# Forty-six chunks of 502 or 504 columns in place of fifty of 470 or 423 in a spectral layer and network on one Trainium2 core

## The chip, the cores and the metric

The kernel runs on one core of a Trainium2 chip. The metric is device time in microseconds (us), the median of several executions. The engines are TensorE (PE, its weight loads apart as PEld), VectorE (DVE), ScalarE (ACT), GpSimd (POOL) and the queue of SyncE (SP), which issues most DMAs.

## What is computed

For eight batches of 3008 rows by 256, a real Fourier transform along the rows, a complex linear map with a soft threshold, the transform back, and then a network on each of the 24064 rows:

```python
    X = np.fft.rfft(x, axis=1)
    Yr = Xr @ w_r - Xi @ w_i + b_r
    Yi = Xr @ w_i + Xi @ w_r + b_i
    Yr = np.sign(Yr) * np.maximum(np.abs(Yr) - lam, 0.0)
    Yi = np.sign(Yi) * np.maximum(np.abs(Yi) - lam, 0.0)
    y = np.fft.irfft(Y, n=x.shape[1], axis=1)
    ...
    h = x @ w_in                 # (24064, 256) @ (256, 2048)
    g = h - np.tanh(h)
    return g @ w_out             # (24064, 2048) @ (2048, 256)
```

## The kernel before

The transform of 3008 = 64 x 47 is done by matmuls in stages. Per batch: forward DFT blocks over 47 (`Stacked`: a load `xt`, the split `xs`, matmul L301 into `ps_f`, a copy `st`, a store `a`), then twelve units of the spectrum (`Spectrum`: a load `at`, the DFT over 64 at L360, the linear map at L380, the threshold on DVE, the inverse DFT over 64 at L426 to L428, a store `z`). The last inverse DFT, over 47, belongs to the network's input. Its work comes in groups of five columns of 24 frequencies (`groups`; each batch has 25 such groups and one of three, 208 in all), and a group turns into 5 x 23.5 columns of the network.

Network rows lie along the columns. A `Chunk` c has four consecutive groups, whichever batch they are of: 470 columns, or 423 (padded to 424) where the short group is among them; 52 chunks. For a chunk, `load` brings `zin`, `wave` does the last DFT (L579, into `ps_i`), `fold` makes `yt` from sums and differences (ACT `odd`, two DVE instructions), and `halves` splits `yt` into a rounded part `yh` (ACT, L599) and its rest `yl` (DVE, L600), for each of the two halves t of the 256 features.

The network is 16 steps f per chunk. A step has `up` (L608: six matmuls of 128x128 weights into a bank `h`: low weights by yh, high weights by yh and by yl, for t of 0 and 1), then ACT `th` = tanh(h), DVE `g` = h - th, ACT `gh`, DVE `gl`, and `down` (L639: six matmuls, accumulated over the 16 steps into two banks `o`). `up` runs two steps ahead of `down` (`AHEAD`), and PE's other work goes between. After the last step `store` copies `o` to `ot` and out.

The order: the first batch and 23 network steps of chunks 0 and 1, which alternate, are written out by hand, from `keep_warm` at the start (matmuls that keep PE busy) on. Everything after that is a plan in slots, one per network step: `plan_stacked` and `plan_spectrum` put each batch's stages at slots counted back from the step at which its first chunk is due, and a chunk's `load`, `time` (wave and fold) and `halves` get slots 2, 8 to 12 and one later. Within this part the framework may still move an instruction ahead on its engine where its inputs and buffers allow. The four banks of `ps_f` are shared by DFT work, and while chunk 1 runs, its two `o` are among them. `zin` has two buffers, as have `xt`, `yh` and `yl`.

Of the kernel before, what the change touches and what calls it, by code (L numbers as in the profile page):

```python
# [10 lines left out]
F32 = mybir.dt.float32  # L11
# [67 lines left out]
def spectral_ffn(ctx, tc, x, w_r, w_i, b_r, b_i, w_in, w_out, x_twice, f1, f1s, f2, i1, i2, out):  # L79
    nc = tc.nc  # L80
# [4 lines left out]
    CT = 470  # L85
# [448 lines left out]
    pieces = [(b, g) for b in range(B) for g in range(NG)]  # L534
# [5 lines left out]
    class Chunk:  # L540
        def __init__(self, c):
            self.c, self.out = c, sizes[c] * 47
            self.n = self.out + self.out % 2
            self.groups = members[c]
# [4 lines left out]
        def load(self):  # L549
            self.tile()  # L550
            k = 0
            while k < len(self.groups):
                b, g = self.groups[k]
                n = sum(q[0] == b and groups[q[1]] == groups[g] for q in self.groups[k:])
# [10 lines left out]
        def time(self, t):  # L565
            self.wave(t)
            self.fold(t)

        def wave(self, t):
            if t == 0:  # L570
                self.yh = work.tile([P, 2, PITCH], F32R, name="yh", tag="yh")
                self.yl = work.tile([P, 2, PITCH], F32R, name="yl", tag="yl")
                self.ps, self.y = {}, {}
            ps = self.ps[t] = ps_f.tile([P, 512], F32, name="ps_i2", tag="f")
            at = 0
            for k, (_, g) in enumerate(self.groups):
                m = groups[g] * NJ
                turn = (g % 2 if m == GR else 2) * GR
                nc.tensor.matmul(  # L579
                    ps[:, at:at + m], self.zt[:m, k, t * P:(t + 1) * P], i2t[:m, turn:turn + m], start=True, stop=True,  # L580
                )
                at += m

        def fold(self, t):
            n = self.n
            v = self.ps[t][:, :sizes[self.c] * 2 * NJ].rearrange("p (n r c) -> p n r c", r=2, c=NJ)
            odd = work.tile([P, D], F32, name="odd", tag="odd")
            ov = odd[:, :sizes[self.c] * NJ].rearrange("p (n c) -> p n c", c=NJ)
# [4 lines left out]
            yv = y[:, :self.out].rearrange("p (n c) -> p n c", c=47)  # L593
            nc.vector.tensor_tensor(out=yv[:, :, :NJ], in0=v[:, :, 0], in1=ov, op=ALU.add)
            nc.vector.tensor_tensor(out=yv[:, :, NJ:], in0=v[:, :, 0, 1:], in1=ov[:, :, 1:], op=ALU.subtract)

        def halves(self, t):
            n, y = self.n, self.y[t]
            nc.scalar.copy(out=self.yh[:, t, :n], in_=y[:, :n])  # L599
            nc.vector.tensor_tensor(out=self.yl[:, t, :n], in0=y[:, :n], in1=self.yh[:, t, :n].bitcast(F32), op=ALU.subtract)  # L600

        def up(self, f, between=()):
# [41 lines left out]
        def store(self):  # L644
            n = self.n
            ot = work.tile([P, 2, 512], F32, name="ot", tag="ot", bufs=1)
            if self.c == NCH - 1:
                lo, n, half = begin[self.c] * 47, self.out, self.n // 2
# [8 lines left out]
            lo, n = begin[self.c] * 47, self.out  # L657
# [5 lines left out]
    with tc.manual_schedule(engines={E.PE, E.Activation, E.DVE, E.Pool, E.SP}):  # L663
# [5 lines left out]
        def keep_warm(n):  # L669
            idle = ps_h.tile([P, 512], F32, name="idle", tag="h")  # L670
            for _ in range(n):
                nc.tensor.matmul(idle, warm[:, :P], warm, start=True, stop=True)

        keep_warm(8)
# [23 lines left out]
        keep_warm(25)  # L698
# [94 lines left out]
        for c in range(2):  # L793
            chunks[c].load_part(LATE, GR)
# [32 lines left out]
        for c in range(2):  # L827
            for t in range(2):
                chunks[c].time(t)
# [61 lines left out]
    def plan_spectrum(units, start, each, ahead, lag, rest):  # L891
        for jp, s in enumerate(units):
            at = start + int(jp * each)
            early = at - jp % 2 * each if units is not second else at
# [12 lines left out]
    whole = set()  # L907
    plan_stacked(1, 25, 1.75, 3, 2 * LOOK)
    plan_spectrum(second, 46, 2.95, 5, 2, 0)
    for b in range(2, B):  # L910
        end = NF * (next(c for c in range(NCH) if begin[c] + sizes[c] > b * 2 * NP) - 1)
        plan_stacked(b, end - 103, 1.75, 3)
        plan_spectrum([Spectrum(b, jp) for jp in range(NJ // 2)], end - 66, 5, 5, 2, 2)
    for c in range(2, NCH):
        at = NF * (c - 1)
        put(at + {2: 9, 6: 6}.get(c, 2), chunks[c].load)
# [50 lines left out]
```

## Time and profile before

| | us |
|---|---|
| median of 3 runs | 2639.81 |
| lowest, highest | 2638.63, 2640.34 |
| span of the profiled execution | 2637.2 |
| PE busy | 2629.1 |
| PEld busy | 2382.4 |
| DVE busy | 1872.5 |
| ACT busy | 1511.3 |
| POOL busy | 115.5 |

The span goes from the first to the last instruction of the profiled execution; the runs' times contain a little more around it. Busy time is a union of instruction times. Since matmuls are pipelined, the duration of one (370 ns for 470 columns) is more than its share of PE's time, which is the distance from its start to the next start.

### The profile page before, as it was taken

The page shows a single profiled execution, that of the slowest core. Times are in us where ns is not written, and L with a number is a line of the kernel's source. Part 1 is how long each engine was busy: PE and PEld are TensorE (multiplying, and loading weights), DVE is VectorE, ACT ScalarE, POOL GpSimd, SP SyncE. Part 2 cuts the span into 40 slices and gives each one's busy share as a digit, 9 for nine tenths or more (in the row PEclk, how much of TensorE's full clock was granted, in tenths as well). Part 3 has the DMA queues.
Part 4 walks back from the last instruction along what each step waited for, and adds up shares of the span by engine and source line. Part 5 has one row for each costly group of instructions (what it writes and reads, how often), then busy time and mean ns, then how long its engine had stood idle before and what let it go on. Part 6 is the DMA issues. An engine that isn't in the chain of part 4 may idle for free.

```text
span 2637.2 us, 38594 instructions
## 1 busy us (share of the span) xinstructions
PE 2629.1 (100%) x14098; PEld 2382.4 (90%) x14098; DVE 1872.5 (71%) x3431; ACT 1511.3 (57%) x2958; POOL 115.5 (4%) x131
## 2 busy tenths in 40 slices
PE   9999999999999999999999999999999999999999
PEld 7789999999999998999999999999999899999888
DVE  5896887677767776767776777667777677755555
ACT  4675558555665556755576555675558555545444
POOL 2110000000000000010000000000000000000000
PEclk9999999999999999999999999999999999999999
DMA  7543326322462213632155221462316422111000
GB/s 240 171 141 92 79 69 193 77 65 62 123 163 69 69 43 80 180 80 67 47 153 138 72 64 38 117 160 59 78 40 180 103 71 63 32 28 29 22 15 15
DMA packets 157543, 236.70 MB, mean 90 GB/s; under 512 B 12561, under 2 KB 108585, under 8 KB 157353
## 3 DMA queue, kind: packets, MB, share of 16 engines
q1 hardware_dynamic: 146025, 213.79, 28.2%
q0 software_dynamic: 11328, 20.45, 5.2%
q8 instruction: 111, 1.82, 0.3%
q14 instruction: 79, 0.65, 0.1%
HBM read 138.77 MB, written 95.42 MB: 89 GB/s over the span
## 4 chain that ended last, share of the span: by engine, by line
PE 96%; DVE 2%; DMA 1%; ACT 1%; issue 0%; SPq 0%; DVEq 0%; ACTq 0%
PE o L639 38%; PE h L608 38%; PE ps_v L380 5%; PE ps_i L579 3%; PE ps_f L360 3%; PE ps_t L380 2%; PE ps_f L301 2%; PE ps_i L428 1%; PE ps_i L427 1%; PE ps_i L426 1%; PE ps_v L482 1%; DMA xt<-in_x 1%; DVE gl L626 0%; PE ps_i L530 0%; ACT gh L623 0%
## 5 line engine op out<-in xcount | busy, mean ns | idle before, releaser
L620 DVE TENSOR_TENSOR g<-h,th 128x470 f32<-128x470 f32 (+1 forms) x832 | 530.8, 638 | 389.0 <-ACT th L617 381.8
L617 ACT ACTIVATE th<-h 128x470 f32<-128x470 f32 (+1 forms) x832 | 462.7, 556 | 588.0 <-PE h L608 584.6
L626 DVE TENSOR_TENSOR gl<-g,gh 128x470 fp32r<-128x470 f32 (+1 forms) x832 | 534.2, 642 | 260.5 <-ACT gh L623 250.2
L623 ACT CAST gh<-g 128x470 fp32r<-128x470 f32 (+1 forms) x832 | 483.7, 581 | 365.7 <-DVE g L620 362.1
L639 PE MATMUL o<-gh,wout_l 128*128 128x470 f32 (+1 forms) x1664 | 624.7, 375 | 0.0
L639 PE MATMUL o<-gl,wout_h 128*128 128x470 f32 (+1 forms) x1664 | 616.8, 371 | 0.0
L639 PE MATMUL o<-gh,wout_h 128*128 128x470 f32 (+1 forms) x1664 | 616.0, 370 | 0.0
L608 PE MATMUL h<-yh,win_l 128*128 128x470 f32 (+1 forms) x1664 | 483.4, 371 | 0.8 <-DVE g L620 0.6
L608 PE MATMUL h<-yl,win_h 128*128 128x470 f32 (+1 forms) x1664 | 482.1, 370 | 0.0
L608 PE MATMUL h<-yh,win_h 128*128 128x470 f32 (+1 forms) x1664 | 480.2, 370 | 0.0
L608 PEld LDWEIGHTS h<-yh,win_l 128*128 128x128 f32 x1664 | 311.7, 188 | 37.7 <-DVE g L620 3.0
L639 PEld LDWEIGHTS o<-gl,wout_h 128*128 128x128 f32 x1664 | 312.7, 188 | 36.3 <-DVE gl L626 1.8
L608 PEld LDWEIGHTS h<-yl,win_h 128*128 128x128 f32 x1664 | 312.6, 188 | 32.6 <-DVE yl L600 0.3
L639 PEld LDWEIGHTS o<-gh,wout_h 128*128 128x128 f32 x1664 | 313.2, 188 | 31.8
L608 PEld LDWEIGHTS h<-yh,win_h 128*128 128x128 f32 x1664 | 312.6, 188 | 32.4
L639 PEld LDWEIGHTS o<-gh,wout_l 128*128 128x128 f32 x1664 | 313.5, 188 | 31.3 <-DVE ot L656 0.2
L296 DVE TENSOR_TENSOR xs<-xt,xs 47x512 fp32r<-47x512 f32 x208 | 139.8, 681 | 41.2 <-ACT xs L295 38.6
L411 DVE TENSOR_TENSOR y<-tb,ps_v 64x256 f32<-64x256 f32 x384 | 160.2, 417 | 7.1 <-ACT tb L498 3.1
L347 POOL DMA_DIRECT2D at<-a x84 | 79.8, 991 | 1780.6 <-DMA at<-a 879.6
L295 ACT CAST xs<-xt 94x512 fp32r<-94x512 f32 x208 | 127.9, 626 | 9.6 <-DMA xt<-in_x_twice 9.3
L304 ACT COPY st<-ps_f 96x512 f32<-96x512 f32 x208 | 117.7, 578 | 1.1 <-PE ps_f L301 1.0
L579 PEld LDWEIGHTS ps_i<-i,zin 120*128 120x128 f32 (+1 forms) x832 | 99.4, 192 | 3.3 <-ACT st L304 0.9
(114 smaller groups left out, 2440.3 us busy)
## 6 DMA issues: line engine op xcount, KB each, us to landing
xt<-in_x_twice SPq DMA_DIRECT2D x104, 384.0 KB
a<-st SPq DMA_DIRECT2D x104, 384.0 KB
at<-a SPq DMA_DIRECT2D x96, 256.0 KB
z<-zo SPq DMA_DIRECT2D x93, 240.0 KB
out<-ot SPq DMA_DIRECT2D x44, 470.0 KB
zin<-z SPq DMA_DIRECT2D x42, 480.0 KB
at<-a POOLq DMA_DIRECT2D x72, 256.0 KB, 5.1
turn<-in_i SPq DMA_DIRECT2D x96, 128.0 KB
```

The source lines that it names most:

```text
L295: nc.scalar.copy(out=xs, in_=src)
L296: nc.vector.tensor_tensor(out=xs[:47], in0=src[:47], in1=xs[:47].bitcast(F32), op=ALU.subtract)
L304: nc.scalar.copy(out=self.st[:, 2 * q:2 * q + 2, :], in_=pv)
L380: nc.tensor.matmul(dst, lhs[:, t], rhs[:, t, :], start=n == 0, stop=n == 5)
L411: nc.vector.tensor_tensor(out=y[ri * 64:(ri + 1) * 64, jj, :], in0=common(jj, ri), in1=self.side(ri)[jj * 64:(jj + 1) * 64], op=ALU.add,)
L579: nc.tensor.matmul(ps[:, at:at + m], self.zt[:m, k, t * P:(t + 1) * P], i2t[:m, turn:turn + m], start=True, stop=True,)
L608: nc.tensor.matmul(h[:, :n], lhs[:, t, f * P:(f + 1) * P], rhs[:, t, :n], start=k == 0, stop=k == 5)
L617: nc.scalar.activation(out=th[:, :n], in_=h[:, :n], func=AF.Tanh)
L620: nc.vector.tensor_tensor(out=g[:, :n], in0=h[:, :n], in1=th[:, :n], op=ALU.subtract)
L623: nc.scalar.copy(out=gh[:, :n], in_=g[:, :n])
L626: nc.vector.tensor_tensor(out=gl[:, :n], in0=g[:, :n], in1=gh[:, :n].bitcast(F32), op=ALU.subtract)
L639: nc.tensor.matmul(self.o[t][:, :n], lhs[:, f, t * P:(t + 1) * P], rhs[:, :n], start=f == 0 and k == 0, stop=f == NF - 1 and k == 2,)
```

## The change

From chunk 2 on, chunks are no longer made of whole groups. The last DFT's work is now a class of its own, `Wave`: up to four groups of one batch, seven waves per batch, 56 in all (the seventh has two groups, 188 columns). The 23124 columns after the first two chunks are divided evenly by `edge` into 46 chunks of 502 or 504. A chunk takes its columns from the two or three waves that it overlaps (`parts`), and `halves` makes `yh` and `yl` piece by piece. A wave's `yt` lives until the next chunk has taken the rest of it, so waves take turns over four homes, three of them buffers of the weight preparation. A wave is loaded at slot 2 of the chunk that first needs it, or four slots earlier if another follows for the same chunk. The batches' stages are planned against the load of the batch's first wave, with forward blocks every 1.6 slots for 1.75 and units every 4.6 for 5. The warm-up of 25 matmuls of 512 columns becomes 40 of mixed shapes with as many columns in all. `th` and `g` get 512 columns of room.

```diff
-    members = [pieces[k:k + 4] for k in range(0, len(pieces), 4)]
+    members = [[(b, g) for g in range(k, min(k + 4, NG))] for b in range(B) for k in range(0, NG, 4)]
     sizes = [sum(groups[g] for _, g in m) // 2 for m in members]
-    begin = [sum(sizes[:c]) for c in range(len(sizes))]
-    NCH = len(sizes)
+    begin = [47 * sum(sizes[:w]) for w in range(len(sizes) + 1)]
+    NCH = 48
+    rest = begin[-1] - begin[2]
+    edge = begin[:2] + [begin[2] + 2 * round(rest * c / (2 * (NCH - 2))) for c in range(NCH - 1)]
...
+    class Wave:
+        def __init__(self, w):
+            self.w, self.groups = w, members[w]
+            self.home = ((work, "yt"), (cvt, "w_f"), (cvt, "w_s"), (cvt, "w_m"))[w % 4 if w > 1 else 0]
...
-            y = self.y[t] = work.tile([P, PITCH], F32, name="yt", tag="yt")
-            if n > self.out:
-                nc.gpsimd.memset(y[:, self.out:n], 0.0)
+            pool, tag = self.home
+            y = self.y[t] = pool.tile([P, PITCH], F32, name="yt", tag=tag)
...
+    class Chunk:
+        def __init__(self, c):
+            self.c, self.lo, self.hi = c, edge[c], edge[c + 1]
+            self.n = self.hi - self.lo
+            self.parts = [w for w in waves if begin[w.w] < self.hi and begin[w.w + 1] > self.lo]
...
         def halves(self, t):
-            n, y = self.n, self.y[t]
-            nc.scalar.copy(out=self.yh[:, t, :n], in_=y[:, :n])
-            nc.vector.tensor_tensor(out=self.yl[:, t, :n], in0=y[:, :n], in1=self.yh[:, t, :n].bitcast(F32), op=ALU.subtract)
+            for w in self.parts:
+                lo, hi = max(self.lo, begin[w.w]), min(self.hi, begin[w.w + 1])
+                y = w.y[t][:, lo - begin[w.w]:hi - begin[w.w]]
+                yh, yl = (v[:, t, lo - self.lo:hi - self.lo] for v in (self.yh, self.yl))
+                nc.scalar.copy(out=yh, in_=y)
+                nc.vector.tensor_tensor(out=yl, in0=y, in1=yh.bitcast(F32), op=ALU.subtract)
...
-        keep_warm(25)
+        keep_warm((8, P, P, 512), (16, P, P, P), (5, 94, 96, 512), (5, 94, P, 512), (6, P, P, D))
...
+    whole, asked, new = set(), {}, {}
+    for c in range(2, NCH):
+        new[c] = [w for w in chunks[c].parts if w.w > 1 and w not in asked]
+        last, apart = (9, 1) if c == 2 else (2, 4)
+        for k, w in enumerate(reversed(new[c])):
+            asked[w] = NF * (c - 1) + last - apart * k
...
-        plan_stacked(b, end - 103, 1.75, 3)
-        plan_spectrum([Spectrum(b, jp) for jp in range(NJ // 2)], end - 66, 5, 5, 2, 2)
+        end = asked[waves[b * len(waves) // B]] - 2
+        plan_stacked(b, end - 95, 1.6, 3)
+        plan_spectrum([Spectrum(b, jp) for jp in range(NJ // 2)], end - 61, 4.6, 5, 2, 2)
...
-        slot = at + (12 if c == 2 else next((k for k in range(8, 13) if at + k in whole), 10))
+        last = NF * (c - 1) + 12
+        for w in new[c]:
+            put(asked[w], w.load)
+            near = range(asked[w] + 6, min(asked[w] + 11, last + 1))
+            slot = asked[w] + 3 if c == 2 else next((k for k in near if k in whole), near[len(near) // 2])
+            for t in range(2):
+                put(slot, w.time, t)
         for t in range(2):
-            put(slot, chunks[c].time, t)
             put(slot + 1, chunks[c].halves, t)
```

Three places in the order of instructions. The first is on PE, in the last steps of chunks 0 and 1, where the last DFT for chunk 2 is done. Names: `h` and `o` are the network's banks, `ps_f` a forward block, `ps_i` the last DFT. Before:

```order
L608 MATMUL h<-yl,win_h 128x470 x2
L301 MATMUL ps_f_1808<-xs,f_stack 96x512
L579 MATMUL ps_i_1817<-i_261,zin 128x120 x4
L639 MATMUL o_1045<-gh,wout_l 128x470
L579 MATMUL ps_i_1827<-i_261,zin 128x120 x4
L639 MATMUL o_1045<-gh,wout_h 128x470
```

And now:

```order
L300 MATMUL ps_f_1795<-xs,f_stack 96x512
L571 MATMUL ps_i_1804<-i_276,zin 128x120 x4
L645 MATMUL o_1090<-gh,wout_l 128x470
L571 MATMUL ps_i_1814<-i_276,zin 128x120 x4
...
L300 MATMUL ps_f_1845<-xs,f_stack 96x512
L571 MATMUL ps_i_1852<-i_276,zin 128x120 x4
L645 MATMUL o_1060<-gh,wout_l 128x470
L571 MATMUL ps_i_1862<-i_276,zin 128x120 x4
```

One forward block and one wave shared a step; now two neighbouring steps have a forward block and a wave each.

The second place is on ACT, at a chunk start whose `yh` stands last. Before, at the start of chunk 10 (the first `th` below is the last of chunk 9):

```order
L617 ACTIVATE th<-h 128x470
L599 CAST yh<-yt 128x470 x2
L623 CAST gh<-g 128x470
L617 ACTIVATE th<-h 128x470
L623 CAST gh<-g 128x470
```

And now, at the start of chunk 6 (446 columns are of chunk 6, 24 of chunk 7, both from the same wave):

```order
L605 CAST yh<-yt 128x446
L605 CAST yh<-yt 128x24
L623 ACTIVATE th<-h 128x502
L303 COPY st<-ps_f_4445 96x512
L303 COPY st<-ps_f_4449 96x512
L629 CAST gh<-g 128x502
L605 CAST yh<-yt 128x446
L303 COPY st<-ps_f_4487 96x512
L294 CAST xs<-xt 94x512 x2
L623 ACTIVATE th<-h 128x504
```

Where both `yh` came behind the last `th` of the chunk ahead, the first now comes in front of it; the 58 columns that chunk 6 has from the older wave were made a chunk earlier, as the 24 of chunk 7 are here.

The third is on the queue of SP, where the loads for chunks 3 and 4 are issued. Before:

```order
L290 DMA xt<-in_x_twice 96x1024 x2
L307 DMA a_648<-st 96x4x256
L557 DMA zin<-z_236 120x4x256
L290 DMA xt<-in_x_twice 96x1024
L307 DMA a_648<-st 96x4x256
L658 DMA out<-ot 128x2x470
```

And now:

```order
L289 DMA xt<-in_x_twice 96x1024 x2
L306 DMA a_663<-st 96x4x256
L557 DMA zin<-z_251 120x4x256 x2
L289 DMA xt<-in_x_twice 96x1024
L306 DMA a_663<-st 96x4x256
L664 DMA out<-ot 128x2x470
```

Two waves' loads stand ahead of the next `xt` where one stood.

## Rows read from the trace of the kernel before

**Rows 1.** The page: busy time of each engine; the chain's shares by engine.
```profile
PE 2629.1 (100%) x14098; PEld 2382.4 (90%) x14098; DVE 1872.5 (71%) x3431; ACT 1511.3 (57%) x2958; POOL 115.5 (4%) x131
...
PE 96%; DVE 2%; DMA 1%; ACT 1%; issue 0%; SPq 0%; DVEq 0%; ACTq 0%
```
**Rows 2.** Waits of PE: who <- for whom: us in total, times, longest.
```profile
PE idle L672 <- DVE column L676: 2.0, 1, 2.0
...
PE ps_i L579 <- ACT st L304: 0.6, 1, 0.6
```
**Rows 3.** Windows: stretch, us, busy PE, PEld, DVE, ACT, POOL, PEclk, DMA share, GB/s.
```profile
1400.00:1700.00 300.00, 300.00 (x1640) 272.94 (x1639) 211.66 (x391) 162.52 (x320) 11.83 (x14) 1.00 0.29 75
...
2290.00:2630.00 340.00, 340.00 (x1714) 311.49 (x1713) 194.27 (x326) 167.06 (x305) 0.39 (x4) 1.00 0.07 22
```
**Rows 4.** Groups by shape, network matmuls, one kind of each line: xcount | busy, mean ns.
```profile
L639 PE MATMUL o<-gh,wout_l 128*128 128x470 f32 x1408 | 533.0, 379 | 0.0
...
L608 PE MATMUL h<-yh,win_h 128*128 128x470 f32 x1408 | 410.3, 373 | 0.0
...
L639 PE MATMUL o<-gh,wout_l 128*128 128x424 f32 x256 | 91.6, 358 | 0.0
...
L608 PE MATMUL h<-yh,win_h 128*128 128x424 f32 x256 | 69.9, 354 | 0.0
```
**Rows 5.** The chain in order of time, tail: start us, us, what.
```profile
2498.99 1.78 PE ps_i L579 x16
...
2541.11 1.78 PE ps_i L579 x16
```
**Rows 6.** Timeline of PE in the last chunk: start us, us, instruction, xcount.
```profile
2600.83 0.55 PE L608 MATMUL h<-yh,win_l 128*128 128x424 f32 x2
...
2605.43 0.55 PE L608 MATMUL h<-yh,win_l 128*128 128x424 f32 x2
```
**Rows 7.** Timeline of PE in the warm-up, a long and a short window.
```profile
21.66 4.04 PE L672 MATMUL idle<-warm 128*128 128x512 f32 x17
...
21.66 0.62 PE L672 MATMUL idle<-warm 128*128 128x512 f32 x2
```
**Rows 8.** Groups by shape, halves of a chunk: xcount | busy, mean ns | idle before.
```profile
L600 DVE TENSOR_TENSOR yl<-yt,yh 128x470 fp32r<-128x470 f32 x88 | 55.6, 644 | 2.2 <-ACT yh L599 0.5
...
L599 ACT CAST yh<-yt 128x470 fp32r<-128x470 f32 x88 | 50.2, 585 | 16.2 <-DVE yt L595 16.0
...
L600 DVE TENSOR_TENSOR yl<-yt,yh 128x424 fp32r<-128x424 f32 x16 | 9.2, 594 | 0.6 <-ACT yh L599 0.3
...
L599 ACT CAST yh<-yt 128x424 fp32r<-128x424 f32 x16 | 8.8, 548 | 4.3 <-DVE yt L595 4.3
```
**Rows 9.** Waits for yh; the timeline of PEld at the start of chunk 10.
```profile
PEld h L608 <- ACT yh L599: 2.9, 8, 0.5
...
597.84 0.19 PEld L608 LDWEIGHTS h<-yh,win_l 128*128 128x128 f32 x1 [0.32 <-ACT yh L599]
```
**Rows 10.** Timeline where the last DFT of chunk 2 is done.
```profile
177.65 0.62 ACT L295 CAST xs<-xt 94x512 fp32r<-94x512 f32 x1 [0.86 <-DMA xt<-in_x_twice]
...
179.73 1.15 PE L579 MATMUL ps_i<-i,zin 120*128 120x120 f32 x8 [0.62 <-ACT st L304]
```
**Rows 11.** Waits of ACT for the loads of forward blocks.
```profile
ACT xs L295 <- DMA xt<-in_x_twice: 9.3, 18, 1.4
```
**Rows 12.** Timeline of PE behind the warm-up.
```profile
26.09 2.02 PE L360 MATMUL ps_f<-f,at 128*128 128x128 f32 x16 [0.17 <-issue]
...
31.72 1.13 PE L360 MATMUL ps_f<-f,at 128*128 128x128 f32 x8 [0.40 <-DMA at<-a]
```
**Rows 13.** Timeline of the end.
```profile
2632.82 0.51 ACT L649 COPY ot<-o 128x423 f32<-128x423 f32 x1 [1.19 <-PE o L639]
```
**Rows 14.** Timeline of PE at a forward block in the chunk from about 715 us.
```profile
722.36 0.40 PE L301 MATMUL ps_f<-xs,f_stack 94*96 94x512 f32 x1
...
722.60 0.36 PE L639 MATMUL o<-gh,wout_l 128*128 128x424 f32 x1
```

More of the change, by code (lines that the diff above doesn't have):

```diff
@@ L533, in spectral_ffn @@
     NG = len(groups)
-    pieces = [(b, g) for b in range(B) for g in range(NG)]
-    members = [pieces[k:k + 4] for k in range(0, len(pieces), 4)]
+    members = [[(b, g) for g in range(k, min(k + 4, NG))] for b in range(B) for k in range(0, NG, 4)]
     sizes = [sum(groups[g] for _, g in m) // 2 for m in members]
-    begin = [sum(sizes[:c]) for c in range(len(sizes))]
-    NCH = len(sizes)
[L540 to L544, printed above, removed]
+    begin = [47 * sum(sizes[:w]) for w in range(len(sizes) + 1)]
[6 more added lines that the diff above has]
+            self.home = ((work, "yt"), (cvt, "w_f"), (cvt, "w_s"), (cvt, "w_m"))[w % 4 if w > 1 else 0]
+            self.ps, self.y = {}, {}
         def tile(self):
@@ L553, in load @@
                 b, g = self.groups[k]
-                n = sum(q[0] == b and groups[q[1]] == groups[g] for q in self.groups[k:])
+                n = sum(groups[q[1]] == groups[g] for q in self.groups[k:])
                 m = groups[g] * NJ
@@ L647, in store @@
             if self.c == NCH - 1:
-                lo, n, half = begin[self.c] * 47, self.out, self.n // 2
+                lo, half = self.lo, n // 2
                 nc.scalar.copy(out=ot[:, 0, :n], in_=self.o[0][:, :n])
@@ L656, in store @@
             nc.vector.tensor_copy(out=ot[:, 1, :n], in_=self.o[1][:, :n])
-            lo, n = begin[self.c] * 47, self.out
+            lo = self.lo
             nc.sync.dma_start(out=out[:, :, lo:lo + n].rearrange("t p n -> p t n"), in_=ot[:, :, :n])
@@ L667, in spectral_ffn, with keep_warm @@
         nc.vector.tensor_copy(out=warm, in_=zero)
-        def keep_warm(n):
+        def keep_warm(*shapes):
             idle = ps_h.tile([P, 512], F32, name="idle", tag="h")
-            for _ in range(n):
-                nc.tensor.matmul(idle, warm[:, :P], warm, start=True, stop=True)
-        keep_warm(8)
+            for times, k, m, n in shapes:
+                for _ in range(times):
+                    nc.tensor.matmul(idle[:m, :n], warm[:k, :m], warm[:k, :n], start=True, stop=True)
+        keep_warm((8, P, P, 512))
         for k, v in enumerate((-LAM, 1150 * 2.0**23, 254 * 2.0**23)):
@@ L773, in spectral_ffn @@
         for c in range(2):
-            chunks[c].tile()
-            chunks[c].load_part(0, LATE)
+            waves[c].tile()
+            waves[c].load_part(0, LATE)
         u10.common()
@@ L793, in spectral_ffn @@
         for c in range(2):
-            chunks[c].load_part(LATE, GR)
+            waves[c].load_part(LATE, GR)
         order = ((1, 2), (1, 3), (2, 0), (2, 1), (2, 2), (2, 3), (3, 0), (3, 1), (3, 2), (3, 3))
@@ L828, in spectral_ffn @@
             for t in range(2):
-                chunks[c].time(t)
+                waves[c].time(t)
             for t in range(2):
@@ L893, in plan_spectrum @@
             at = start + int(jp * each)
-            early = at - jp % 2 * each if units is not second else at
+            early = start + int((jp - jp % 2) * each) if units is not second else at
             put(early - ahead, s.load)
```

30 lines of the change are left out of this document (12 added, 18 removed).

## The prediction

> **What bounds the kernel now.** The page comes first. TensorE (PE) is busy in 2629.1 of 2637.2 us, and the chain that ended last lies on it for 96% [rows 1]. Busy is no proof, since matmuls overlap, so the waits of PE come next: its longest is 2.0 us at the start, and the one that lies in the planned part of the program is 0.6 us [rows 2]. The windows by stage say the same place by place: in 1400 to 1700 us PE is busy in all 300 us, VectorE (DVE) in 212, ScalarE (ACT) in 163, at a granted clock of 1.00, which is the upper level, 2.4 GHz; in the last stage, with the spectral work gone, PE is still full and DVE at 57% [rows 3]. So from about 190 us to the end the time is the sum of the starts of one matmul to the next, and other engines count only where they make PE wait. What the change does to that sum is the question.
>
> How many of these matmuls are network? The groups by shape give 1408 of each of the six kinds at 470 columns and 256 of each at 424 [rows 4]: 8448 + 1536 = 9984 of 14098 records, 192 for each of 52 chunks.
>
> **What one costs, by its width.** Durations (about 370 ns) are of no use here; the distance between starts is. In the tail the last DFT's matmuls recur once per chunk of 470 columns, at 2498.99 and 2541.11 us: 42.12 us, of which 16 records of that DFT take 1.78 [rows 5]. So 192 network matmuls take 40.34 us, 210.1 ns each. In the last chunk, of 424 columns, 24 matmuls lie between 2600.83 and 2605.43: 191.7 ns each, 36.80 us for a chunk [rows 6]. Wider than 470 there is only the warm-up, 128x128 weights and 512 columns: 17 take 4.04 us, 2 take 0.62, so (4.04 - 0.62) / 15 = 228.0 ns [rows 7]. From 424 to 470 a column costs 18.4 / 46 = 0.400 ns, from 470 to 512 it costs 17.9 / 42 = 0.426. A column at 2.4 GHz would be 0.417, between the two. On this line 210.1 ns is 196 for the columns and 14 that each matmul pays whatever its width. That 14 is what fewer matmuls can save.
>
> The Trainium skill, "TensorE: Matmul & The Clock Gate", section "Back-to-back issue gap", gives the warm gap as columns / 2.4 + 2.5 ns. These rows do not agree: they show 14 ns above the columns [rows 5 to 7]. By the figure of the Trainium skill 768 matmuls fewer would be worth an estimated 1.9 us, by the rows more than 10.
>
> **The change part by part.** *Fewer, wider matmuls.* Chunks 2 to 51 are 42 of 470 and 8 of 424; now 46 of 502 or 504, mean 23124 / 46 = 502.7. That is 192 x 4 = 768 matmuls fewer, and the 8 padded columns are gone. Before: 42 x 40.34 + 8 x 36.80 = 1988.7 us. After: at 0.426 ns a column 210.1 + 32.7 x 0.426 = 224.0 ns, at 0.400 it is 223.2; I take the middle, 223.6, because one end is an interpolation to a row outside the network and the other an extrapolation within it. 46 x 192 x 223.6 ns = 1974.8 us: **-13.9 us**, between -10.3 (224.0) and -17.4 (223.2).
>
> *Last DFT apart from the chunks.* 56 waves instead of 52, but the same 208 groups and so the same PE records (832 of them, 1.78 us per 16 [rows 5]): 0 on PE. The few more ACT and DVE instructions of the four extra waves lie beside PE.
>
> *Halves in pieces.* A chunk is now cut out of two or three waves, so its yh and yl are made by 4 or 6 instructions on each engine instead of 2 (200 instead of 104 in all, by the order). Over 46 columns yh differs by 37 ns and yl by 50 [rows 8], which leaves about 210 and 130 ns per instruction whatever its width: 96 x 0.21 = 20 us more on ACT, 96 x 0.13 = 12 us more on DVE, spread over 2400 us in which they are idle for over a quarter. Cover: PE, two network steps ahead. If that cover were gone, a chunk start would pay 0.4 us. Where the cover is thin shows in the trace: PE's weight load waits for yh at a chunk start, 0.32 us at 597.84, and 2.9 us in 8 waits over the run [rows 9]. These are chunks whose yh stands right ahead of their first matmul. By the order there were six of these besides chunk 2 and there are four now (6, 8, 14, 20), and half of their pieces are already done, since the piece of the older wave is made a chunk earlier (order of ACT). I take 0, between -1 and +2 us.
>
> *Two waves for chunk 2.* It needs waves 2 and 3 in neighbouring steps, where chunk 1 still holds two of the four banks of ps_f. Before, the one wave there made PE wait 0.62 us for ACT's st copy; ACT itself had been held for 0.86 by a late xt load [rows 10]. Now there are two such places (order of PE), and on SP one more zin load stands ahead of the next xt load (order of SP). Behind ACT's waiting xs copy its tanh of the next step is queued, for which DVE's g and then PE wait. +0.6 us, between 0 and +1.9 (three times what the one place costs).
>
> *A tighter plan.* Forward blocks come every 1.6 steps instead of 1.75, spectral units every 4.6 instead of 5. A step of 12 matmuls grows from 12 x 210.1 = 2.52 us to 2.68, so in time the distances are 4.29 us instead of 4.41 and 12.3 instead of 12.6, that is 2 to 3% closer, and the waits of ACT for xt, 9.3 us in 18 places [rows 11], grow. Little of that reaches PE now [rows 2]. +0.5 us, between 0 and +3.
>
> *Warm-up.* 40 matmuls with the same 12,800 columns instead of 25: 15 x 14 ns = +0.2 us; if the 16 narrow ones take 111 ns like the DFT's [rows 5], +0.9. PE goes from there to the first spectral matmul with a gap of 0.17 us, but the third unit then waits 0.40 us for its load [rows 12], which takes in the first part. +0.2, between 0 and +0.9.
>
> *The end.* The last chunk's copy out (0.51 us for 423 columns [rows 13]) has 502 columns: +0.1 us. The memsets of the padded column on GpSimd go: nobody waited for them, 0.
>
> Sum: -13.9 + 0 + 0.6 + 0.5 + 0.2 + 0.1 = -12.5 us. The profiled execution has a span of 2637.2, so 2624.7; the median of the runs, 2639.81, lies 2.6 above that span, and so the forecast is **2627.3 us**. All good ends together give -18.3 (2621.5), all bad ones -2.4 (2637.4).
>
> **The rivals.** *Slower: wide matmuls cost more inside the network than in the warm-up.* The only 512-column matmuls between network matmuls, the forward DFT's, take 0.24 us from 722.36 to 722.60 [rows 14], not 0.228. Were this what width costs there, a column above 470 would be (240 - 210.1) / 42 = 0.71 ns, 502.7 columns 233.4 ns, and 8832 of them 2061 us, +72: with the other terms 2714 us. It decides from 225.0 ns on, where gain and small costs cancel. For it: it is the nearest neighbour in place and width. Against it: those matmuls have other weights (94 rows, 96 columns) and change shape at both sides, while the network's at 470 lie on one line with the warm-up's to 1 ns. Chance 0.08.
>
> *No change: a matmul costs by its columns alone.* At 210.1 / 470 = 0.447 ns a column 502.7 columns take 224.7 ns, 8832 of them 1984.6 us, only -4.1; with +1.4 this is 2637.1, within 0.2%. Against it: the price of a column falls with width, 0.452 at 424, 0.447 at 470, 0.445 at 512 [rows 5 to 7]; but the last step of that fall is small. Chance 0.10. (The small fixed part in the Trainium skill, "TensorE: Matmul & The Clock Gate", "Back-to-back issue gap", would lead to this side too.)
>
> *The gain is there and waits take half of it.* The tighter forward blocks make ACT late at most of some 100 loads, or the xt loads meet the zin loads at a batch's border, and 7 batches pay 1 us each: 2634, on the border of what can be told. For it: 9.3 us of ACT waits now. Against it: only 0.6 us of them came through to PE. Chance 0.15, half of it faster, half the same.
>
> **How the numbers follow.** A measurement of this kernel can tell about 0.2%, 5.3 us, from no change. Forecast with its bounds 0.67, all of it faster; half of the waits rival 0.08: faster 0.75. Same: 0.07 + 0.10 = 0.17. Slower: 0.08. The range goes from all good ends, 2621, to all bad ends and the column rival, 2637; outside is the slower case and a little at the edges.
>
> **What would show it.** Right: 46 x 192 network matmuls; in the tail the last DFT's matmuls recur after 192 x 0.2236 + 1.78 = 44.7 us where a whole wave falls in; 12 matmuls of a step in 2.68 us; PE's waits still a few us in all; DVE and ACT shares as before. Wrong in its main term: a step of over 2.70 us (225 ns each). Wrong in the small ones: new rows with PE or its weight load waiting for yh at chunk starts, for xs in the forward stages, or for st near 175 to 190 us.

## The result: slower by 0.7%, and the profile after

The changed kernel takes 2658.05 us (median of 4 runs, 2657.47 to 2659.17) against 2639.83 us (median of 4): ratio 1.0069, 95% interval 1.0055 to 1.0084. The forecast was 2627.3 us, faster, with a range up to 2637: wrong in sign and outside the range. The profiled execution, the slowest of the four, has a span of 2657.4 us, 20.2 more than before. One of the ten executions of a later run (distance 256) took 7608 us and is left out of its ratio.

The page of the changed kernel, busy time and chain, answers to [rows 1]:
```profile
PE 2646.9 (100%) x13345; PEld 2245.9 (85%) x13345; DVE 1868.8 (70%) x3411; ACT 1505.8 (57%) x2930; POOL 114.1 (4%) x115
...
PE 95%; DVE 1%; ACT 1%; DMA 1%; issue 0%; SPq 0%; POOL 0%; DVEq 0%; ACTq 0%; POOLq 0%
```
PE has 753 records fewer and is busy 18 us longer; it is still what bounds the kernel, and the shares of DVE and ACT are those of before. The changed kernel's waits (who <- for whom: us in total, times, longest): those of PE, as [rows 2], those of ACT for loads, as [rows 11], and those of PE's weight load for yh, as [rows 9]:
```profile
PE idle L679 <- DVE column L683: 2.0, 1, 2.0
PE ps_f L359 <- DMA at<-a: 1.3, 1, 1.3
PE h L614 <- DVE g L626: 0.6, 1, 0.6
...
PE ps_i L571 <- ACT st L303: 0.5, 1, 0.5
```
```profile
ACT xs L294 <- DMA xt<-in_x_twice: 2.6, 4, 1.2
```
```profile
PEld h L614 <- ACT yh L605: 1.0, 2, 0.5
```
So no wait took the gain: PE's waits are 5.6 us in all where they were 4.0, ACT's waits for xt fell from 9.3 us to 2.6, and the weight load's for yh from 2.9 to 1.0. What is left is the price of the matmuls themselves. Windows of the changed kernel, as [rows 3], say that PE is full at the upper clock as before:
```profile
1400.00:1700.00 300.00, 300.00 (x1549) 257.25 (x1548) 213.48 (x394) 168.10 (x332) 11.61 (x12) 1.00 0.33 85
2290.00:2650.00 360.00, 360.00 (x1661) 301.64 (x1660) 201.53 (x335) 170.94 (x308) 0.00 (x0) 1.00 0.08 23
```
The groups by shape, as [rows 4], confirm the counts: 960 x 6 = 30 chunks of 502 and 512 x 6 = 16 of 504 columns, 192 matmuls each.
```profile
L614 PE MATMUL h<-yh,win_h 128*128 128x502 f32 x960 | 297.3, 391 | 0.0
...
L614 PE MATMUL h<-yh,win_h 128*128 128x504 f32 x512 | 157.4, 388 | 0.0
```
Now the price, read as in [rows 5] (the chain, tail: start, us, what) and [rows 6] (the timeline of PE, 24 matmuls of 504 columns apart):
```profile
2459.73 1.78 PE ps_i L571 x16
...
2505.24 1.78 PE ps_i L571 x16
...
2550.83 1.78 PE ps_i L571 x16
```
```profile
2601.04 0.61 PE L614 MATMUL h<-yh,win_l 128*128 128x504 f32 x2
...
2606.48 0.62 PE L614 MATMUL h<-yh,win_l 128*128 128x502 f32 x2
```
(45.51 - 1.78) / 192 = 227.8 (54 of these matmuls have 504 columns, the others 502) and (45.59 - 1.78) / 192 = 228.2 ns, where 223.6 was forecast; 5.44 / 24 = 226.7 ns at 504. From the third chunk on, the mean distance from one network matmul's start to the next is 227.9 ns at 502 and 227.0 at 504, mean 227.6; in the kernel before it is 210.7 at 470 and 192.2 at 424. (Counted are neighbours of the same line; distances over 260 ns, nearly all of them right behind other DFT matmuls, are left out. Such a mean moves by some 0.2 ns with what is counted.) So the network from the third chunk on takes 8832 x 227.6 = 2010.2 us against 8064 x 210.7 + 1536 x 192.2 = 1994.3: **+15.9 us**. In these two executions the first network step also comes 2.7 us later, the extra wave beside chunk 2 costs 0.6 and the end 0.4. Together this is 19.6 of the 20.2 us. A check without means: from the first step of chunk 2 to the last network matmul 2463.1 us pass where it was 2448.4, with one wave (1.78 us) less among them, so the matmuls and the plan together take 16.5 us more.

### The profile page after: what moved, and what is told of

It is laid out like the page before. It is cut to its first block, busy times and chain, and to the rows that moved or that the text cites. A ratio compares the mean times of both kernels' runs of the same rounds, so it can differ in the third digit from the quotient of the medians.

```text
span 2657.4 us, 36886 instructions
## 1 busy us (share of the span) xinstructions
PE 2646.9 (100%) x13345; PEld 2245.9 (85%) x13345; DVE 1868.8 (70%) x3411; ACT 1505.8 (57%) x2930; POOL 114.1 (4%) x115
## 4 chain that ended last, share of the span: by engine, by line
PE 95%; DVE 1%; ACT 1%; DMA 1%; issue 0%; SPq 0%; POOL 0%; DVEq 0%; ACTq 0%; POOLq 0%
PE o L645 38%; PE h L614 38%; PE ps_v L379 5%; PE ps_i L571 3%; PE ps_f L359 3%; PE ps_t L379 2%; PE ps_f L300 2%; PE ps_f L251 1%; PE ps_i L425 1%; PE ps_i L427 1%; PE ps_i L426 1%; PE ps_v L481 1%; DMA xt<-in_x_twice 1%; DVE gl L632 0%; PE ps_i L529 0%; ACT gh L629 0%
## 5 line engine op out<-in xcount | busy, mean ns | idle before, releaser
L626 DVE TENSOR_TENSOR g<-h,th 128x502 f32<-128x502 f32 (+2 forms) x768 | 521.1, 678 | 425.3 <-ACT th L623 420.8
L623 ACT ACTIVATE th<-h 128x502 f32<-128x502 f32 (+2 forms) x768 | 452.8, 590 | 613.6 <-PE h L614 607.7
L632 DVE TENSOR_TENSOR gl<-g,gh 128x502 fp32r<-128x502 f32 (+2 forms) x768 | 523.9, 682 | 258.1 <-ACT gh L629 241.9
L629 ACT CAST gh<-g 128x502 fp32r<-128x502 f32 (+2 forms) x768 | 471.2, 614 | 339.7 <-DVE g L626 336.5
L645 PE MATMUL o<-gh,wout_l 128*128 128x502 f32 (+2 forms) x1536 | 606.0, 395 | 0.0
L645 PE MATMUL o<-gl,wout_h 128*128 128x502 f32 (+2 forms) x1536 | 598.1, 389 | 0.0
L645 PE MATMUL o<-gh,wout_h 128*128 128x502 f32 (+2 forms) x1536 | 597.0, 389 | 0.0
L614 PE MATMUL h<-yh,win_l 128*128 128x502 f32 (+2 forms) x1536 | 475.0, 389 | 0.8 <-DVE g L626 0.6
L614 PE MATMUL h<-yh,win_h 128*128 128x502 f32 (+2 forms) x1536 | 473.4, 389 | 0.0
L614 PE MATMUL h<-yl,win_h 128*128 128x502 f32 (+2 forms) x1536 | 473.4, 389 | 0.0
```

The source lines that it names most:

```text
L614: nc.tensor.matmul(h[:, :n], lhs[:, t, f * P:(f + 1) * P], rhs[:, t, :n], start=k == 0, stop=k == 5)
L626: nc.vector.tensor_tensor(out=g[:, :n], in0=h[:, :n], in1=th[:, :n], op=ALU.subtract)
L629: nc.scalar.copy(out=gh[:, :n], in_=g[:, :n])
L632: nc.vector.tensor_tensor(out=gl[:, :n], in0=g[:, :n], in1=gh[:, :n].bitcast(F32), op=ALU.subtract)
L645: nc.tensor.matmul(self.o[t][:, :n], lhs[:, f, t * P:(t + 1) * P], rhs[:, :n], start=f == 0 and k == 0, stop=f == NF - 1 and k == 2,)
```

## Experiments

The distances below are means over the network matmuls of a width in that trace, as above. A "train" is a row of equal matmuls, and "distance in bytes" is how far the first byte of the moving columns lies from that of the weights in each partition, modulo 512. Each ratio is against the kernel before on the same chip.

**Quiet trains.** Is it the width? In place of the changed kernel's warm-up stand trains of 24 equal matmuls, with the other engines all but idle; nothing else is changed, and the total grows.
```
-        keep_warm((8, P, P, 512), (16, P, P, P), (5, 94, 96, 512), (5, 94, P, 512), (6, P, P, D))
+        keep_warm((24, P, P, 512))
+        keep_warm(*((24, P, P, n) for n in (256, 384, 416, ..., 510, 512)))
+        keep_warm(*((24, P, P, n, 8) for n in (470, 488, 496, 502, 504)))
...
```
The 8 makes the columns begin 8 elements, 32 bytes, further on.

> The changed kernel with its warm-up replaced by trains of 24 matmuls each (128x128 weights, one train per width: 256, 384, 416, 424, ... 470, 472, 480, 484, 488, 490, ... 512 columns), while the other engines have next to nothing to do; then some widths again from a start 8 columns further on, and some with 94 rows or 96 weight columns. Only PE's distances between starts are read, the total grows by about 200 us. In the changed kernel the network's matmuls of 502 columns start 227.9 ns apart, those of 504 226.9, where the line through 424, 470 and 512 gave 223.6. Theory A, the width itself: a matmul of 502 or 504 columns costs what one of 512 does, so cost goes in steps, and the quiet trains show it too: 502 and 504 within 1.5 ns of 512 (226 to 228), and a flat stretch of some width below 512. Theory B, the company: alone, 502 columns lie on the line, 222.5 to 223.7, and what is above comes from the network's other work. Theory C, the start addresses: the trains from another start differ by 3 ns or more from those at the tile's start.


470 columns took 213.1 ns, 502 took 223.8, 504 and 512 both 226.6; with the columns 32 bytes further on, 470 took 210.5, 502 took 228.0 and 504 took 226.7, within 0.3 ns the network's values. So the cost is no line in the width, and it depends on where the operands lie. I drew from it that steps of some 6.7 ns per 16 columns count, and the columns' own place; both had to be tested.

**Other widths in the network**: 47 chunks of 492 columns; five of 502 or 504, then 40 of 512 and a rest of 130; later 50 of 462 or 464, with the warm-up of before.
```
-    NCH = 48
+    NCH = 49
```
```
-    edge = begin[:2] + [begin[2] + 2 * round(rest * c / (2 * (NCH - 2))) for c in range(NCH - 1)]
+    edge = begin[:2] + [begin[2] + 2 * round(rest * c / (2 * (NCH - 2))) for c in range(6)]
+    edge += [min(edge[-1] + 512 * (c + 1), begin[-1]) for c in range(NCH - 7)]
```
```
-    NCH = 48
+    NCH = 52
```


> One number changed: 47 chunks of 492 columns each instead of 46 of 502 or 504. Theory A (steps by width): if 492 lies on the flat stretch with 512, 47 x 192 matmuls at 227 ns are 2049 us against 2019.6 now, +29: about 2687. If it lies on the line below the stretch, 219.3 ns, 1979 us, -41: about 2617. Theory B (company, about 4 ns on every width above 470): 223.5 ns, 2017 us: about 2655. The forecast's own line would be the 2617.

> Chunks 2 to 6 as in the changed kernel, then 40 chunks of 512 columns and a last one of 130. Theory A: 512 columns cost what 502 do, 228 ns, so the columns above 502 are free: 5 x 192 x 227.6 + 40 x 192 x 228 = 1969.5, the last chunk 192 x about 0.08 to 0.11 = 15 to 21 us, in all 1985 to 1991 against 2019.6: about 2624 to 2630, faster than the kernel before. Theory B: 512 costs 232 in the network: 2000 + 18, about 2656, no change against the changed kernel.

> The changed kernel with 50 chunks of 462 or 464 columns from the third on instead of 46 of 502 or 504, and the warm-up of the kernel before. Theory 'the cost of a matmul goes in steps of about 6.7 ns for each 16 columns begun': 464 columns are 29 times 16, 31 steps or 206.7 ns; 9600 x 206.7 = 1984 us against 8064 x 210.5 + 1536 x 192.2 = 1993 us in the kernel before, less the cost of the tighter plan and the extra wave (about +2 us): 2631 to 2634 us. Rival 'proportional to columns, 0.4535 ns each as at 502 and 504': 210 ns, 2016 us: about 2665 us. Rival 'as the quiet trains of 464 had it, 208.7 ns': 2004 us, about 2653 us.


492: 2664.95 us, 1.0094 (1.0079 to 1.0109), 223.5 ns. 512: 2676.81 us, 1.0140 (1.0125 to 1.0155), 233.2 ns. 462 and 464: 2649.34 us, 1.0036 (1.0023 to 1.0049), 207.7 and 211.0 ns. The timeline of PE with 512 columns, 24 matmuls apart, (2605.29 - 2599.69) / 24 = 233.3:
```profile
2599.69 0.63 PE L615 MATMUL h<-yh,win_l 128*128 128x512 f32 x2
...
2605.29 0.63 PE L615 MATMUL h<-yh,win_l 128*128 128x512 f32 x2
```
The same 512 columns take 226.6 in the train. None of these widths made the whole kernel faster than 470 and 424 do, and the idea of steps of 16 columns fell with 464 (211.0, not 206.7).

**The warm-up of before in the changed kernel** (25 matmuls of 512 columns).
```
-        keep_warm((8, P, P, 512), (16, P, P, P), (5, 94, 96, 512), (5, 94, P, 512), (6, P, P, D))
+        keep_warm((25, P, P, 512))
```


> The changed kernel with the old warm-up, 25 matmuls of 512 columns. The start of the network's first step came 2.7 us later in the changed kernel than before (100.2 against 97.5), of which 1.0 at the first spectral matmul. If the longer warm-up is the cause, the first step is back at 97.5 to 98 and the time at 2655.5; if it was the loads' chance in one execution, the first step stays or moves by itself and the median stays at 2658.


2657.57 us, 1.0067 (1.0050 to 1.0084), 0.5 us less than the changed kernel: not the cause of the loss. The first network step came 2 us earlier (98.27 instead of 100.22 us), but that can't be put down to the warm-up. In the runs below, kernels with the new warm-up reach that step between 97.2 and 100.0 us, and those with the old one between 97.2 and 99.9. The third spectral unit's wait for its load differs too, from 0 to 1.4 us with the new warm-up and from 0.2 to 1.9 with the old. Its first matmuls in the kernel before with weights moved (old warm-up), and in the changed kernel at distance 256 (new warm-up):
```profile
33.90 1.13 PE L362 MATMUL ps_f<-f,at 128*128 128x128 f32 x8 [1.86 <-DMA at<-a]
...
31.27 1.13 PE L361 MATMUL ps_f<-f,at 128*128 128x128 f32 x8
```

**The columns moved by 32 bytes.** In the built programs of before and after, win and wout begin at a multiple of 64 bytes in each partition, the columns (yh, yl, gh, gl) 32 bytes past one; the distance of columns from weights is 32 modulo 512 (the tile sizes in the code add up to the same). The const tile "gap" stands between them.
```
-        const.tile([P, 64], F32, name="gap")
+        const.tile([P, 72], F32, name="gap")
```
It was done to the changed kernel, the kernel before, the one with 512 columns, and a mixture of 20 chunks of 512 and 26 of 496 (warm-up of before).


> The changed kernel with the unused tile between the network's weights and all later tiles widened by 8 columns (32 bytes), so that the moving tiles yh, yl, gh, gl start at a multiple of 64 bytes as the weights do. Place of the operands counts (R or L): 502 columns go from 227.9 to about 223.8 ns, 504 stay at 226.7: 5760 x -4.1 = -24 us, about 2634. Place does not count in the network (the 228 comes from its other work): 2658, no change.

> The kernel before with the same 32 bytes of shift. Place counts: 470 columns go from 210.6 to about 213.1 ns, 8064 x 2.5 = +20 us, and 424 from 192.2 to 193.3, +1.7: about 2661, slower than before by what the change itself cost. Place does not count: 2640.

> The kernel with 40 chunks of 512 columns (233.4 ns there) and the 32 bytes of shift. Place counts: 512 columns at 226.6 as in the quiet train, 7680 x -6.8 = -52 us, and the five of 502 and 504 -3: about 2622, faster than the kernel before. Place does not count: 2677.

> From chunk 2 on 20 chunks of 512 and 26 of 496 columns (the last 484), the 32 bytes of shift and the old warm-up. If the network follows the quiet trains with weights and moving columns at the same place, 512 columns cost 226.6 and 496 cost 220.0 ns: 20 x 192 x 226.6 + 26 x 192 x 220.0 = 1968 us against 2020 in the changed kernel, -51, and -0.5 for the warm-up: about 2606, faster than both. If place does not count, 233.4 and about 224: 2014 us, about 2652.


Changed kernel: 2659.69 us, 1.0074 (1.0057 to 1.0091), 227.3 and 228.8 ns. Kernel before: 2663.2 us, 1.0088 (1.0073 to 1.0103): 23 us for 32 bytes. 512: 2649.32, 1.0034 (1.0021 to 1.0047), 229.4 ns, 27 us less. Mixture: 2658.79, 1.0073 (1.0056 to 1.0089), 230.3 and 226.4 ns. The chain in the tail of the kernel before so moved, (42.75 - 1.78) / 192 = 213.4 ns where [rows 5] gave 210.1:
```profile
2479.15 1.78 PE ps_i L579 x16
...
2521.90 1.78 PE ps_i L579 x16
```
Place counts, but not so that columns at a multiple of 64 bytes, as the weights are, would be good: the changed kernel and the mixture missed what the trains gave.

**Trains by place of both operands**: weights and columns shifted by (0, 0), (8, 0), (0, 8), (8, 8), (0, 4), (0, 2) elements.
```
-        keep_warm((8, P, P, 512), (16, P, P, P), (5, 94, 96, 512), (5, 94, P, 512), (6, P, P, D))
+        keep_warm((24, P, P, 512))
+        for w, o in ((0, 0), (8, 0), (0, 8), (8, 8), (0, 4), (0, 2)):
+            keep_warm(*((24, P, P, n, w, o) for n in (424, 470, 488, 492, 496, 502, 504)))
```


> The changed kernel with trains of 24 quiet matmuls in place of the warm-up, for 424, 470, 488, 492, 496, 502 and 504 columns, each with the start of the weights and that of the moving columns at (0, 0), (8, 0), (0, 8), (8, 8), (0, 4), (0, 2) columns from the tile's start; the tile itself starts 32 bytes behind a multiple of 64. Only the distances are read. In the network the weights start at a multiple of 64 bytes and the moving tiles 32 behind one. In the first trains 8 columns of shift turned 470 from 213.1 to 210.5 ns, 496 from 220.0 to 224.4, 502 from 223.8 to 228.0, and the shifted values are the network's. Theory R, the relation: it counts whether weights and moving columns start alike: (0, 0) and (8, 8) give the first values, (8, 0) and (0, 8) the second. Theory L, the moving columns' own place: (8, 0) is like (0, 0), and (8, 8) like (0, 8).


The timeline of PE, a long and a short window of one train each: 470 columns (0, 8) and (8, 8), 502 columns (0, 8) and (8, 8).
```profile
104.98 4.15 PE L680 MATMUL idle<-warm 128*128 128x470 f32 x19
104.98 0.79 PE L680 MATMUL idle<-warm 128*128 128x470 f32 x3
141.23 4.64 PE L680 MATMUL idle<-warm 128*128 128x470 f32 x21
141.23 0.59 PE L680 MATMUL idle<-warm 128*128 128x470 f32 x2
126.03 4.72 PE L680 MATMUL idle<-warm 128*128 128x502 f32 x20
126.03 0.61 PE L680 MATMUL idle<-warm 128*128 128x502 f32 x2
162.71 4.41 PE L680 MATMUL idle<-warm 128*128 128x502 f32 x19
162.71 0.61 PE L680 MATMUL idle<-warm 128*128 128x502 f32 x2
```
470: (4.15 - 0.79) / 16 = 210.0 ns with the columns 32 bytes past the weights, (4.64 - 0.59) / 19 = 213.2 at distance 0. 502: (4.72 - 0.61) / 18 = 228.3 and (4.41 - 0.61) / 17 = 223.5. What is good for 470 is bad for 502. With distance 8, 16 or -32 bytes 470 took 216.1, 216.4 and 213.3 (means of whole trains). But two trains of one width at the same place differ by up to 5.3 ns (488 columns at distance 0: 220.0 in the first run of trains, 225.3 in this one), so a train alone is no price for a network.

**Weights moved.** This parts "the columns' own place" from "the distance between the two". In the kernel before, with gap 32 the network's weights move by 32 bytes and its columns stay (distance 0); with gap 40 the columns move by 32 too (distance 32 again). The small tiles between weights and gap (`column`, `f2`, `bias`) move by 128 bytes in both.
```
+    const.tile([P, 8], F32, name="lead")
     win_h = const.tile([P, 2, FF], F32R, name="win_h")
...
     wout_l = const.tile([P, NF, D], F32R, name="wout_l")
+    const.tile([P, 24], F32, name="trail")
...
-        const.tile([P, 64], F32, name="gap")
+        const.tile([P, 32], F32, name="gap")
```


> The kernel before with only the four network weight tiles moved by 32 bytes, so that weights and moving columns both begin 32 bytes past a multiple of 64 (in the kernel before the weights begin at a multiple of 64, the moving columns 32 bytes past one). Theory 'the moving columns' own place sets the cost' : the moving columns have not moved, so 470 columns stay at 210.5 ns and the time at 2640 us. Rival 'the place of the weights against the columns sets it': this is the same relation as in the run that moved the columns to a multiple of 64, so 470 columns take 213.3 ns and the time is about 2663 us.

> The kernel before with the weight tiles moved by 32 bytes and the moving columns moved by 32 bytes too, so that the two are again 32 bytes apart but the columns begin at a multiple of 64. Theory 'the moving columns' own place sets the cost': 213.3 ns and about 2663 us, as in the run that moved the columns alone. Rival 'the place of the weights against the columns': 210.5 ns and about 2640 us.


Distance 0: 2662.62 us, 1.0085 (1.0069 to 1.0102), 213.4 ns. Distance 32, both elsewhere: 2639.88 us, 1.0003 (0.9993 to 1.0012), 210.6 ns. The rival, the distance between the two, holds in both: moving the columns along with the weights changed nothing. Chains of the tail, where no spectral work is left, 42.75 (first) and 42.12 us (second, the same as [rows 5]) from one to the next:
```profile
2479.40 1.78 PE ps_i L581 x16
...
2522.15 1.78 PE ps_i L581 x16
```
```profile
2457.64 1.78 PE ps_i L581 x16
...
2499.76 1.78 PE ps_i L581 x16
```

**The same for the changed kernel and the other widths**: distance 0 with gap 32 as above, 128 with gap 64, 256 with gap 96. The 512, mixture and 492 kernels have the warm-up of before.


> The changed kernel with nothing but its weight tiles moved by 32 bytes, so that weights and columns begin at the same place modulo 512 bytes. Theory 'modulo 64': 227.2 ns at 502 and 228.7 at 504 columns as with the columns moved, about 2659 us. Rival 'distance 0 does as the quiet trains', 223.5 and 227.0 ns: some (30 x 3.7 + 16 x 1.7) x 192 = 27 us less, about 2632 us, the forecast nearly met. If 227.9 and 226.9 ns stay as they are, 2658 us.

> The kernel with 40 chunks of 512 columns, its weight tiles moved by 32 bytes, so that weights and columns begin at the same place modulo 512 bytes, as in the quiet trains; warm-up of the kernel before. Theory 'the distance modulo 64 bytes is all that counts': as the run with the columns moved, 229.5 ns and about 2649 us. Rival 'the distance counts over more than 64 bytes, and at distance 0 the network does as the quiet trains': 226.6 ns, 7680 x 2.9 = 22 us less, about 2627 us.

> The mixture of 20 chunks of 512 and 26 of 496 columns, weight tiles moved by 32 bytes so that weights and columns begin at the same place modulo 512 bytes. Theory 'modulo 64': as with the columns moved, 230.4 and 226.6 ns, about 2659 us. Rival 'distance 0 does as the quiet trains', 226.6 and 220 to 223 ns: (20 x 3.8 + 26 x 3.6 to 6.6) x 192 = 33 to 48 us less, 2611 to 2626 us.

> The version with 47 chunks of 492 columns, weight tiles moved by 32 bytes so that weights and columns begin at the same place modulo 512 bytes, warm-up of the kernel before. Quiet trains of 492 at this place took 219.9 and 222.2 ns; in the network, 32 bytes apart, it was about 224 ns and 2665 us. Rival 'distance 0 does as the quiet trains': 47 x 192 x 2 to 4 ns = 18 to 36 us less, 2629 to 2647 us. Theory 'wide matmuls in the network stay dearer than in trains, whatever the place': 223 ns or more, 2656 us or more.

> The changed kernel, with its weights 128 bytes from the columns modulo 512 (0 in the run before, 32 in the changed kernel, 64 with the columns moved). Theory 'the distance counts modulo 128 bytes': 224.4 and 227.2 ns at 502 and 504 columns, about 2639 us. Theory 'it counts over more than 128 bytes, and only distance 0 is cheap': as at 64 bytes, 227.3 and 228.7 ns, about 2659 us.

> The changed kernel, with its weights 256 bytes from the columns modulo 512. Theory 'modulo 128' or 'modulo 256': about 2639 us. Theory 'only distance 0 modulo 512 is cheap': about 2659 us.

| kernel, distance in bytes | us | ratio (95%) | ns per matmul |
|---|---|---|---|
| changed, 32 (as given) | 2658.05 | 1.0069 (1.0055 to 1.0084) | 227.9 / 227.0 |
| changed, 64 (columns moved) | 2659.69 | 1.0074 (1.0057 to 1.0091) | 227.3 / 228.8 |
| changed, 128 | 2665.64 | 1.0098 (1.0081 to 1.0115) | 226.7 / 232.2 |
| changed, 0 | 2639.07 | 0.9996 (0.9986 to 1.0005) | 224.5 / 227.2 |
| changed, 256 | 2638.21 | 0.9992 (0.9983 to 1.0002) | 224.5 / 227.2 |
| 40 x 512, 0 | 2637.63 | 0.9991 (0.9981 to 1.0000) | 228.2 |
| 512 and 496, 0 | 2637.00 | 0.9989 (0.9979 to 0.9998) | 228.3 / 223.1 |
| 492, 0 | 2649.80 | 1.0039 (1.0025 to 1.0053) | 222.1 |

Moving the weights took 19 us off the changed kernel. The spectral matmuls, some of whose operands move along, hardly change (DFT over 64: 111.7 ns from start to start in both; linear map: 119.1 and 118.5). Distance 0 and 256 are alike; 128 gives the longest time of this kernel, by its 504 columns alone, since 502 cost less there than at 32. So the distance counts over more than 128 bytes, and 256 is as good as 0. The chains of the tail at distance 0 (all 502 columns) and at 128 (54 of 504 among them), (44.68 - 1.78) / 192 = 223.4 and (45.63 - 1.78) / 192 = 228.4 ns:
```profile
2486.34 1.78 PE ps_i L573 x16
...
2531.02 1.78 PE ps_i L573 x16
```
```profile
2465.60 1.78 PE ps_i L573 x16
...
2511.23 1.78 PE ps_i L573 x16
```
At distance 0 the tail does as the quiet trains (502 columns: 223.4 in the last stage, trains 223.5 to 224.6), while the stages with spectral work are dearer (224.3 to 225.9). The rival's 2632 us was missed by 7 us, most of it there; what makes a matmul some 1 ns slower in those stages was not tried. No version is faster than the kernel before by more than 0.2%: the best, 0.9989, gains 0.11%.

## Why the prediction was wrong, point by point

- **Bound, counts, clock**: right. PE sets the time, 46 x 192 matmuls, waits of a few us in all, granted clock 1.00.
- **The main term, -13.9 us, is the step that failed; it measured +15.9.** What failed is "the network's at 470 lie on one line with the warm-up's". The line went through two points of the network [rows 5, 6] and one of the warm-up [rows 7]. The warm-up takes weights and columns from the same tile, from its first byte on: distance 0. The network's lie 32 bytes apart. At 32 bytes 512 columns take 233.2 ns in the network, at 0 about 228.2; and 470 at 0 take 213.4 instead of 210.7. So the three points, which fell on a line of 0.40 to 0.43 ns a column, do not belong to one line; that they fell on one looks like chance. On the network's own distance a column above 470 costs (227.6 - 210.7) / 32.7 = 0.52 ns. Of the 30 us by which the term missed, 8832 x (227.6 - 223.6) = 35 lie there, less some 5 because the tail's 210.1 and 191.7 ns were taken for the whole run, where it was 210.7 and 192.2. Not all of the 35 are the distance's: at distance 0 the mean is 225.4, which takes back 19 us, and 8832 x (225.4 - 223.6) = 16 stay. Of these 3072 x (227.2 - 223.6) = 11 are at 504 columns, which cost nearly as much in the quiet trains (226.6), so even at one distance the price follows no line; 5760 x (224.5 - 223.6) = 5 are at 502 columns, in the stages with spectral work, and their cause is open. In the tail at distance 0 the last DFT recurs after 44.68 us, the 44.7 that was named as the sign of being right.
- **"14 ns that each matmul pays whatever its width"**: wrong as a constant. Above the columns at 2.4 GHz, 502 columns pay 223.4 - 209.2 = 14.2 ns in the tail at distance 0 and 227.9 - 209.2 = 18.7 at the kernel's own; 470 pay 213.4 - 195.8 = 17.6 at distance 0 and 210.7 - 195.8 = 14.9 at 32. The figure of the Trainium skill, "TensorE: Matmul & The Clock Gate", section "Back-to-back issue gap", columns / 2.4 + 2.5 ns, which that section calls the gap of an isolated matmul, was not reached by any train or network of 128 columns of weights here; the least gap above the columns at 424 to 512 columns was 13.2 ns (424 columns, 189.9 ns). So the prediction's doubt against that figure held.
- **Rival "wide matmuls cost more inside the network"**: its point of decision (225.0 ns) was passed, and the loss that it foretold came. But its price, 0.71 ns a column and 233.4 ns, was too high for 502 columns, and its mechanism is not width alone: the same 502 columns at distance 0 take 224.5. Its chance of 0.08 was too low for the one rival that the only neighbour within the network spoke for [rows 14].
- **Rival "by its columns alone"** (224.7 ns, 2637 us) is close to what the kernel does at distance 0: 225.4 ns, 2639.
- **Rival "waits take half"**: wrong; ACT's waits for xt fell [rows 11].
- **Halves in pieces, 0**: right; no wait for yh or yl appears among PE's, and its weight load waits 1.0 us in 2 places for yh where it was 2.9 in 8 [rows 9].
- **Two waves for chunk 2, +0.6**: measured +0.6, but the size is luck. From the first network step to the first of chunk 2 it is 89.41 us (100.22 to 189.63) where it was 87.05 (97.51 to 184.56), 2.36 more, and 1.78 of that is the wave itself, which only moved ahead. The wait for st that was priced got shorter, 0.50 us where it was 0.62 [rows 10]. The time went in the second place: there the forward block starts 0.70 us behind the network matmuls ahead of it (182.45) where the first place has 0.42 (177.11), and the wave starts 0.57 behind the block where the first has 0.24. Its weight load waits for ACT, where the yh of chunk 2 is being made:
```profile
177.53 0.40 PE L300 MATMUL ps_f<-xs,f_stack 94*96 94x512 f32 x1
177.77 1.05 PE L571 MATMUL ps_i<-i,zin 120*128 120x120 f32 x8
...
179.53 1.15 PE L571 MATMUL ps_i<-i,zin 120*128 120x120 f32 x8 [0.50 <-ACT st L303]
...
183.15 0.44 PE L300 MATMUL ps_f<-xs,f_stack 94*96 94x512 f32 x1
...
183.69 0.97 PEld L571 LDWEIGHTS ps_i<-i,zin 120*128 120x128 f32 x8 [0.41 <-ACT yh L605]
...
183.72 1.12 PE L571 MATMUL ps_i<-i,zin 120*128 120x120 f32 x8
```
- **Tighter plan, +0.5**: not told apart. The sum leaves 0.6 us, and that is within what the means are good for; ACT's waits for xt fell where they were said to grow.
- **Warm-up, +0.2 (at most 0.9)**: not contradicted. In the profiled executions the first network step is 2.7 us later, but the run with the old warm-up and those with moved weights say that such a difference is between executions. The timeline of PE, as [rows 7, 12]: the first spectral unit starts at 27.08 instead of 26.09, and the third waits 1.29 us for its load instead of 0.40.
```profile
20.05 7.19 PE L679 MATMUL idle<-warm 128*128 128x512 f32 x40
27.08 1.95 PE L359 MATMUL ps_f<-f,at 128*128 128x128 f32 x16
...
33.54 1.13 PE L359 MATMUL ps_f<-f,at 128*128 128x128 f32 x8 [1.29 <-DMA at<-a]
```
  With the old warm-up the median fell by 0.5 us.
- **The end, +0.1**: 0.4 by the trace; the copy of 502 columns takes 0.58 us where 423 took 0.51 [rows 13].

## What to carry to other kernels

A price per column holds only for operands that lie as those of the kernel do: before a width is changed, a few matmuls of the new width are timed with the kernel's own weights and columns, at their own distance. Trains at 32 bytes came within 0.3 ns of the network for 470, 502 and 504 columns, but not for 492 (220.1 in the train, 223.5 in the network), so the whole kernel decides. If a tuned width turns out to be cheap, try the same width with the weights moved by 32 bytes before calling it the width's merit, and after any change of width try the place anew. Here the old widths and the new ones end at the same time (0.9996) when each has its good distance.

## What was not expected of the hardware

- The distance in bytes between where weights and columns begin changes the time from one matmul to the next: 470 columns 210.7 ns at 32, 213.4 at 0 and 64; 502 columns 224.5 at 0 and 256, 227.9 at 32; 504 columns 227.2 at 0 and 232.2 at 128; 512 columns 228.2 at 0 and 233.2 at 32. On the whole kernel this is 19 us (changed kernel, 32 against 0), 23 us (kernel before, 0 or 64 against 32) and 39 us (512 columns: 2676.81 against 2637.63, the latter with the old warm-up).
- 502 columns can cost more than 504 (227.9 against 227.0 at 32 bytes), and 504 and 512 the same in trains (226.6).
- Why is open. Weight loads run beside the matmuls (PEld 85% of the span on the page above), so one thought is that the two get in each other's way; no run took the weight loads away, and it is not shown. What the traces show is that the weight loads themselves do not get longer. With 512 columns, the mean in the last stage (2290 to 2600 us) at distance 32 and at 0 is 187 and 188 ns, while the matmuls' records go from 395 to 389:
```profile
L615 PEld LDWEIGHTS h<-yh,win_l 128*128 128x128 f32 x209 | 39.1, 187 | 9.6
L615 PE MATMUL h<-yh,win_l 128*128 128x512 f32 x210 | 65.9, 395 | 0.0
...
L617 PEld LDWEIGHTS h<-yh,win_l 128*128 128x128 f32 x220 | 41.3, 188 | 8.6
L617 PE MATMUL h<-yh,win_l 128*128 128x512 f32 x219 | 67.5, 389 | 0.0
```
